# Issuing the k and v loads of two chunk pairs from ScalarE's queue in a gated-recurrence and gated-MLP kernel

## Chip, cores and metric

The kernel runs on one NeuronCore of a Trainium2 chip. The metric is the device time of one execution in microseconds. A "load" below is a transfer from the chip's main memory (HBM) into the core's working memory (SBUF); an engine "issues" a load when its instruction queue hands the transfer over, and the load "lands" when the last part of it has arrived.

## What is computed

The reference is a recurrence over time, for 4 batches and 8 heads of width 48, followed by a gated MLP in which the sequence positions are mixed by a 768 x 768 matrix. Cut to what matters:

```python
def _attn_ref(q, k, v, alpha):              # each (4, 8, 768, 48), float32
    state = np.zeros((B, H, D, D))
    for t in range(S):
        state = alpha[:, :, t, :, None] * state + np.einsum('bhd,bhe->bhde', k[:, :, t], v[:, :, t])
        y[:, :, t] = np.einsum('bhd,bhde->bhe', q[:, :, t], state)
    return y

def _moe_ref(x, w_in, w_spatial, b_spatial, w_out):   # x: (4, 768, 384), w_in: (384, 1024)
    h = np.maximum(x @ w_in, 0.0)
    u, v = h[..., :512], h[..., 512:]
    v_n = (v - mean(v)) / np.sqrt(var(v) + 1e-06)
    v_s = np.einsum('ts,bsd->btd', w_spatial, v_n) + b_spatial[None, :, None]
    return (u * v_s) @ w_out                          # (4, 768, 384)
```

`x` is `y` with the heads side by side.

## The kernel before, in words

The sequence of each batch is cut into six chunks of 128 positions, 24 chunks in all. Within a chunk the recurrence becomes matrix products. With a running sum of log(alpha) (`cum`), k is multiplied by exp(-cum) (`kt`, L449 for pairs and L628 for single chunks) and q by exp(cum) (`qt`, L456 and L638); both are transposed by TensorE and copied to SBUF (`kqT`), multiplied with each other into a 128 x 128 score (`pt`), masked by VectorE (`ptm`, L540 and L696), and multiplied with v (`y`, L556 and L713). A state carried from chunk to chunk (`state`, `sbd`) adds what earlier chunks contribute (L562, L707). `y` is then transposed into `xT`, the input of the MLP. The MLP part (all matmuls on L759) multiplies `xT` by the two halves of `w_in`: half 1 gives v, half 0 gives u; v is normalised, mixed by the transposed `w_spatial`, gated with u and multiplied by `w_out`.

The first six chunks, the whole first batch, are handled in three pairs (`PAIRS`, function `pair(j)` with j = 0, 1, 2): two chunks share each load of alpha, q, k and v. A pair's load is 384 KB, in pieces of 96 floats for 128 partitions and 8 heads (L391). In this text ac0, kc0, qc0 and vc0 are the tiles of alpha, k, q and v for pair 0, and so on to ac2, kc2, qc2, vc2. From chunk 6 on, each chunk has four loads of 192 KB (L585). The loads of `w_in` are two transfers of 768 KB each (L986), half 1 first; they arrive in float32 in `raw_w` and are cast to bf16 by ScalarE, VectorE and GpSimd (L191, L193). All loads, and the stores at the end, are issued by SyncE (SP), except for one tiny bias load by GpSimd.

No scheduler is at work when the kernel is built: every operation is numbered, and the text constant `PLAN` lists the numbers in the order in which they are emitted, each with a letter for its engine (P TensorE, D VectorE, A ScalarE, G GpSimd, S SyncE). `replay` (L111) walks through it and calls each operation's `emit`. Each engine runs what was emitted to it in that order, and every engine waits by semaphores for what it needs. The first part of the plan is:

```python
PLAN = """
G32 Q33 G0 S34 S36 Q35 S38 S96 S40 Q37 S98 D1 S100 S166 A42 Q39 S102 D2 S170
P43:384:384:384:384:384:384:384:384:384:384:384:384 S168 G3 Q97 S4 P54:384 A46 A44 S172 A45 S303 G47 A57 A55 D48 Q41
```

S34, S36, S38 and S40 are ac0, kc0, qc0 and vc0; S96, S98, S100 and S102 are ac1, kc1, qc1 and vc1; S166, S168, S170 and S172 are ac2, kc2, qc2 and vc2. S4 is `w_in` half 1, S303 is the alpha load of chunk 6, and the load of `w_in` half 0 is S9 in the next line. A42 is the logarithm of alpha for pair 0 (`la`, L402); P43 and P54 are the running sums of its even and odd positions (`cum`, L413), and on ScalarE A46, A44 and A45 are the three exponentials that follow the first of them: `bc` (L444), `binvp` (L429, exp(-cum), which `kt` needs) and the one in place (L438, exp(cum), which `qt` needs); A57, A55 and A56 are the same for the odd positions. Numbers after a colon are matmuls on dummy data (`junk`, L183).

Every load counts up one of eight completion semaphores, which are handed out in turn; an issue that reuses one first waits until the load that had it before has landed. Three buffers per tile name (`IO = 3`) let all three pairs' loads be issued without waiting for a pair to be used up.

Of the kernel before, what the change touches and what calls it, by code (L numbers as in the profile page):

```python
# [123 lines left out]
def kernel(  # L124
# [12 lines left out]
    nc = tc.nc  # L137
# [235 lines left out]
    def pair(j):  # L373
# [13 lines left out]
        def load(name, src):  # L387
            def emit(_):
                t = st[name] = io_pool.tile([128, 2, H, D], FP32, name=name).rearrange(
                    "p a h d -> p (a h d)").rearrange("p (h a d) -> p h a d", h=H, a=2)  # L390
                nc.sync.dma_start(  # L391
                    out=t.rearrange("p h a d -> p h (a d)"),
                    in_=src[b, :, t0:t0 + 2 * C, :].rearrange("h (p a) d -> p h (a d)", a=2))
            return emit
# [667 lines left out]
```

## Time and profile before

| what | value |
|---|---|
| median of 3 runs | 150.17 us (150.13 to 150.49) |
| the profiled execution | 149.26 us, of which the span from first to last instruction is 147.5 us |
| TensorE (PE) busy | 140.0 us, 95% of the span |
| VectorE (DVE) busy | 121.9 us, 83% |
| ScalarE (ACT) busy | 105.6 us, 72% |
| GpSimd (POOL) busy | 87.1 us, 59% |
| read from HBM, written to HBM | 23.60 MB, 4.72 MB |
| granted TensorE clock | full speed |

The views of the profile used here are: the page's line of busy tenths, which cuts the span in 40 slices and gives one digit for each (9 is 90% or more), with the DMA engines' share and the GB/s below it; the chain of waits, which goes back from the last instruction and names at each step what released it; the timeline of one engine, with start, length, engine, source line and operation; and the list of who waited for whom. On SP's timeline the length of an issue is the time for which SP was held by it, not the time of the transfer. The trace also records when a load landed on each of the 16 DMA engines; the last of them is the landing time in this text.

### The profile page before, as it was taken

The numbers are of one execution on the slowest core, as the hardware profiler recorded it, in microseconds if no ns is written. First come the engines' busy times: TensorE is split into PE (matmuls) and PEld (weight loads), VectorE is DVE, ScalarE is ACT, GpSimd is POOL, SyncE is SP. The second block draws the span as 40 slices with busy tenths as digits, with TensorE's granted clock in tenths as the row PEclk, the third lists the DMA queues.
The fourth block names the chain that finished last, engine by engine and source line by source line (L and its number), as shares of the span: only waits on it lengthen the run. The fifth ranks groups of instructions, "written<-read, shape, count | busy, mean of one in ns | idle before, by whom it ended". The sixth has DMA issues, their size and how long they took to land.

```text
span 147.5 us, 4398 instructions
## 1 busy us (share of the span) xinstructions
PE 140.0 (95%) x1687; PEld 89.8 (61%) x1687; DVE 121.9 (83%) x266; ACT 105.6 (72%) x264; POOL 87.1 (59%) x149
## 2 busy tenths in 40 slices
PE   6899999989998999999999999999999999999990
PEld 3457766546765766667666757665765766555550
DVE  6688978969999998998996789999898969867611
ACT  3577848788958769899967899899956458950160
POOL 6947468296072978852569877858059897004320
PEclk9999999999999999999999999999999999999999
DMA  4999999989999899899996999997949302250154
GB/s 113 267 261 263 261 287 267 311 213 257 293 203 209 173 209 277 159 207 180 211 225 132 207 224 183 258 231 150 251 138 207 63 4 107 107 213 4 70 198 161
DMA packets 93013, 28.60 MB, mean 194 GB/s; under 512 B 87872, under 2 KB 91456, under 8 KB 92992
## 3 DMA queue, kind: packets, MB, share of 16 engines
q1 hardware_dynamic: 92960, 28.32, 82.9%
q8 instruction: 13, 0.21, 0.7%
q14 instruction: 8, 0.07, 0.2%
q0 software_dynamic: 32, 0.00, 0.0%
HBM read 23.60 MB, written 4.72 MB: 192 GB/s over the span
## 4 chain that ended last, share of the span: by engine, by line
PE 79%; DMA 6%; POOL 4%; ACT 3%; DVE 3%; issue 3%; SPq 0%; POOLq 0%
PE ps L759 51%; DMA raw_w<-in_moe_w_in_dram 6%; PE pt L655 6%; PE pt L685 4%; PE tp L671 2%; PE y L346 2%; PE y L713 2%; PE cum L604 2%; POOL mask L243 2%; PE y L707 2%; PE ps L478 1%; PE ps L769 1%; PE ps L413 1%; PE ps L183 1%; ACT xT L191 1%
## 5 line engine op out<-in xcount | busy, mean ns | idle before, releaser
L759 PE MATMUL ps<-w_spT,vn 128*128 128x384 bf16 x192 | 36.2, 326 | 0.0
L912 POOL TENSOR_TENSOR gT<-vsb,uT 128x384 bf16<-128x384 f32 x28 | 25.6, 925 | 15.7 <-DVE vsb L899 15.1
L628 POOL TENSOR_TENSOR kt<-kc,binv 128x384 bf16<-128x384 f32 x18 | 16.4, 912 | 15.3 <-ACT binv L616 14.6
L696 DVE TENSOR_TENSOR ptm<-pt,mask 128x512 bf16<-128x512 f32 x36 | 23.8, 681 | 0.3 <-PE pt L685 0.2
L759 PEld LDWEIGHTS <-vn 128*128 128x128 bf16 x192 | 17.0, 97 | 9.7 <-issue 0.2
L759 PE MATMUL ps<-xT,w_in 128*128 128x384 bf16 x96 | 19.7, 326 | 0.6 <-ACT xT L191 0.4
L899 DVE TENSOR_TENSOR vsb<-ps,bsp_bc 128x384 f32<-128x384 f32 x31 | 16.5, 550 | 3.6 <-PE ps L759 3.2
L759 PE MATMUL ps<-w_in,xT 128*128 128x512 bf16 x72 | 19.5, 379 | 0.0
L759 PE MATMUL ps<-w_out_sb,gT 128*128 128x384 bf16 x96 | 18.4, 326 | 0.0
L317 POOL TENSOR_TENSOR state<-state,bc 128x192 f32<-128x192 f32 x20 | 10.6, 531 | 10.7 <-DVE state L312 7.2
L191 ACT CAST x_sb<-y 128x384 bf16<-128x384 f32 x24 | 11.5, 481 | 6.3 <-PE y L713 5.0
L821 DVE BATCH_NORM_STATS2 stats<-v_sb 128x6 f32<-128x512 bf16 x20 | 13.7, 683 | 1.4 <-ACT v_sb L197 1.4
L191 ACT COPY xT<-y 128x384 bf16<-128x384 bf16 x24 | 11.5, 481 | 4.1 <-PE y L346 3.4
L197 ACT ACTIVATE v_sb<-ps 128x512 bf16<-128x512 f32 x20 | 11.9, 598 | 2.1 <-PE ps L759 2.1
L193 POOL CAST sbd<-state 64x192 bf16<-64x192 f32 x36 | 12.3, 342 | 1.5
L759 PEld LDWEIGHTS <-w_in 128*128 128x128 bf16 x96 | 8.6, 97 | 6.6 <-issue 1.1
L759 PEld LDWEIGHTS <-gT 128*128 128x128 bf16 x96 | 8.9, 98 | 5.7
L638 DVE TENSOR_TENSOR qt<-qc,cum 128x384 bf16<-128x384 f32 x18 | 9.9, 549 | 2.3 <-ACT cum L633 2.0
L193 DVE COPY kqT<-pt 128x1024 bf16<-128x1024 bf16 x14 | 9.6, 687 | 2.3 <-PE pt L655 2.2
L616 ACT ACTIVATE binv<-cum 128x384 bf16<-128x384 f32 x18 | 8.9, 496 | 3.5 <-PE cum L607 2.9
L191 ACT COPY o_sb<-ps 128x384 f32<-128x384 f32 x9 | 4.3, 483 | 8.8 <-PE ps L759 8.6
L851 DVE TENSOR_SCALAR vn<-v_sb,mvs,rstd 128x512 bf16<-128x512 bf16 x24 | 9.6, 428 | 0.2 <-ACT rstd L844 0.2
(131 smaller groups left out, 298.6 us busy)
## 6 DMA issues: line engine op xcount, KB each, us to landing
ac<-in_alpha_dram SPq DMA_DIRECT2D x18, 192.0 KB, 4.3
kc<-in_k_dram SPq DMA_DIRECT2D x18, 192.0 KB, 3.8
qc<-in_q_dram SPq DMA_DIRECT2D x18, 192.0 KB, 3.8
vc<-in_v_dram SPq DMA_DIRECT2D x18, 192.0 KB, 3.9
raw_w<-in_moe_w_spatial_dram SPq DMA_DIRECT2D x3, 768.0 KB, 5.8
out_dram<-raw_w SPq DMA_DIRECT2D x12, 192.0 KB, 2.3
out_dram<-o_sb SPq DMA_DIRECT2D x9, 192.0 KB, 1.9
raw_w<-in_moe_w_in_dram SPq DMA_DIRECT2D x2, 768.0 KB, 7.9
```

Of the source, the lines that this page charges most:

```text
L191: nc.scalar.copy(out=out, in_=in_)
L193: ENG[eng].tensor_copy(out=out, in_=in_)
L197: nc.scalar.activation(out=out, in_=in_, func=AF.Relu)
L317: ENG[eng].tensor_tensor(out=st["state"], in0=st["state"], in1=st["bc"][:, :, None].to_broadcast([128, HP, D]), op=ALU.mult)
L628: ENG[eng].tensor_mul(out=kt[:, :, :, 0:D], in0=quad(st["kc"]), in1=st["binv"])
L638: nc.vector.tensor_mul(out=qt[:, :, :, 0:D], in0=quad(st["qc"]), in1=st["cv"])
L696: nc.vector.tensor_tensor(out=st["ptm"][:, s], in0=st[f"pt{s}"], in1=mask4, op=ALU.mult)
L759: return lambda ps: nc.tensor.matmul(out=out(ps), lhsT=lhsT(), rhs=rhs(), start=start, stop=stop)
L821: nc.vector.bn_stats(out=stats, in_=d["v_sb"][:, tt, :])
L851: nc.vector.tensor_scalar(out=d["vn"][:, t, :], in0=d["v_sb"][:, t, :], scalar1=d["mvs"][:, t, 0:1], scalar2=d["rstd"][:, t:t + 1], op0=AL ...
L899: nc.vector.tensor_tensor(out=hold["vs"], in0=ps[:, 0:TH], in1=bsp_bc[:, th, :], op=ALU.add)
L912: ENG[eng].tensor_tensor(out=bt[b]["gT"][:, dsl, cols], in0=hold["vs"], in1=bt[b]["uT"][:, dsl, cols], op=ALU.mult)
```

## The change

The loads of k and v for pairs 1 and 2 are issued through `nc.scalar`, so that they stand in ScalarE's instruction queue. Pair 0's four loads, and the alpha and q loads of all pairs, stay with SyncE. `PLAN` is not edited: the four words S98, S102, S168 and S172 keep their places, and so each load stands on ScalarE's queue where its word stands among the A words.

```diff
@@ -388,7 +388,7 @@
             def emit(_):
                 t = st[name] = io_pool.tile([128, 2, H, D], FP32, name=name).rearrange(
                     "p a h d -> p (a h d)").rearrange("p (h a d) -> p h a d", h=H, a=2)
-                nc.sync.dma_start(
+                (nc.scalar if j and name in ("kc", "vc") else nc.sync).dma_start(
                     out=t.rearrange("p h a d -> p h (a d)"),
                     in_=src[b, :, t0:t0 + 2 * C, :].rearrange("h (p a) d -> p h (a d)", a=2))
             return emit
```

In the built program ScalarE's queue now begins: table load, kc1, `la` of pair 0 (L402), vc1, kc2, `bc` (L444), `binvp` (L429), vc2, the exponential in place (L438), and then as before. SP's queue begins: ac0, kc0, qc0, ac1, vc0, qc1, ac2, qc2, `w_in` half 1, the alpha load of chunk 6, `w_in` half 0. No other instruction moves on any engine. Because the semaphores are handed out in the order of building, some waits name other loads than before: ac2's issue waits for the landing of kc0, qc2's for qc0, `w_in` half 1's for ac1 (as before), vc2's for kc1, the alpha load of chunk 6 for vc0 and kc2, and that of `w_in` half 0 for vc1 (before: qc1).

## The prediction

> **What bounds the kernel now.** I read the page first, then the chain of waits, then the timelines of SP and ScalarE for the first 30 us, then the list of waits.
>
> The page's busy lines:
>
> ```profile
> span 147.5 us, 4398 instructions
> ...
> PE   6899999989998999999999999999999999999990
> ...
> DMA  4999999989999899899996999997949302250154
> GB/s 113 267 261 263 261 287 267 311 213 257 293 203 209 173 209 277 159 207 180 211 225 132 207 224 183 258 231 150 251 138 207 63 4 107 107 213 4 70 198 161
> ```
>
> A slice is 3.69 us. TensorE is full from the third slice on, but up to about 29 us that includes dummy matmuls (line 183: 3.59 us of 7 to 20 us, 1.22 us of 20 to 30 us, none later). The DMA engines are full from the second slice, at a flat 261 to 267 GB/s while the pairs' loads run. So the opening is bound by bytes, the rest by TensorE.
>
> The chain of waits says where one becomes the other:
>
> ```profile
> 17.91 0.49 ACT binvp L429
> 18.42 0.47 ACT ps L438
> 18.90 0.41 ACT xT L191
> 19.30 0.17 SPq L585
> 19.52 8.84 DMA raw_w<-in_moe_w_in_dram
> 28.38 1.19 DVE w_in L193 x2
> 29.61 0.68 PE ps L759 x3
> ```
>
> The second half of w_in is issued at 19.52, lands at 28.36, is cast, and the u matmuls begin at 29.61. After that TensorE's own waits sum to 1.2 us, so what is late at 29.61 is late at the end, 118 us later.
>
> SP's timeline shows that its issues queue for bytes:
>
> ```profile
> 0.74 0.43 SPq L391 DMA_DIRECT2D ac<-in_alpha_dram  x1
> 1.23 0.57 SPq L391 DMA_DIRECT2D kc<-in_k_dram  x1
> 1.85 1.09 SPq L391 DMA_DIRECT2D qc<-in_q_dram  x1
> ...
> 5.77 1.44 SPq L391 DMA_DIRECT2D kc<-in_k_dram  x1
> 7.25 1.44 SPq L391 DMA_DIRECT2D qc<-in_q_dram  x1
> ...
> 19.52 3.32 SPq L986 DMA_DIRECT2D raw_w<-in_moe_w_in_dram  x1
> ```
>
> The same 384 KB issue takes 0.43 us with nothing ahead of it and 1.44 us from the fourth on, back to back. The landing events give ac0 4.43, kc0 5.96, qc0 7.46, ac1 8.97, vc0 10.48, kc1 11.98, qc1 13.49, ac2 14.96: one load per 1.50 us (384 KB / 1.50 us = 262 GB/s, the page's rate). Then one DMA engine falls behind by about 1.5 us: vc1 has landed on half of them at 16.19, on the last at 17.82; qc2 follows at 19.24, kc2 20.48, w_in's first half 23.09, vc2 24.40.
>
> ScalarE's timeline, where the moved loads will stand:
>
> ```profile
> 4.52 0.84 ACT L402 ACTIVATE la<-ac 128x768 bf16<-128x768 f32 x1 [2.50 <-DMA ac<-in_alpha_dram]
> 6.21 0.17 ACT L444 ACTIVATE bc<-ps 128x4 f32<-128x4 f32 x1 [0.85 <-PE ps L420]
> 6.29 0.48 ACT L429 ACTIVATE binvp<-ps 128x384 bf16<-128x384 f32 x1
> 6.80 0.47 ACT L438 ACTIVATE ps<-ps 128x384 f32<-128x384 f32 x1
> ```
>
> Between la and bc it is idle for 0.85 us; from bc to 8.24 us it is not. Waits for loads, from the list of waits:
>
> ```profile
> POOL vbp L193 <- DMA vc<-in_v_dram: 3.6, 2, 2.0
> ...
> POOL w_in L193 <- DMA raw_w<-in_moe_w_in_dram: 2.9, 1, 2.9
> ...
> DVE qt L456 <- DMA qc<-in_q_dram: 1.4, 1, 1.4
> ```
>
> (total, times, longest). Pair 0 waits for qc0 and vc0, which stay on SP; pair 1 waits for vc1, which moves; and GpSimd waits 2.9 us for w_in's second half.
>
> [...]
>
> **The change, part by part.**
>
> *Removed from SP:* four issues. kc1, vc1 and kc2 took 1.44, 1.39 and 2.62 us and vc2 0.51, so SP comes to the later ones up to 6.0 us sooner. That is worth nothing by itself: the bytes are unchanged and the rate was already full.
>
> *Bytes reordered.* [...]kc1 (issued near 1 us) goes out beside ac0 and kc0, and vc1 and kc2 follow from about 5 us. Every load left on SP is pushed back by the ScalarE loads that overtake it, at 1.50 us each: qc0 by one (7.46 to 9.0), vc0 by two to three (10.48 to 13.5-15), qc1 by three (kc1 was ahead already: 13.49 to 18.0), ac2 by three (14.96 to 19.5; 20.9 if the lagging engine lags as before), w_in's first half by one (vc2 now ahead: 23.09 to 24.6). w_in's second half has the same bytes ahead as before: 28.36. Slack to set against this: qc0 and vc0 none, ac1 1.0 us (la starts at 9.99), qc1 0.8 (qt at 14.27), ac2 1.05 (la at 16.01).
>
> *Added to ScalarE:* four issues. kc1 stands in idle time, before ac0 has landed: nothing but its bytes, which I take as +0.75 us for ac0 (half a load; bounds 0 and 1.5), so la starts at about 5.2. Behind la stand vc1 and kc2; queued behind them are bc, binvp and everything of pair 0, and waiting for those are GpSimd's kt, VectorE's qt and TensorE's transposes. Behind vc2 stand the in-place exponential (qt waits) and the odd positions. Price of one such issue: 0.43 us at least (SP's[...]), 1.44 + 1.44 = 2.9 us at most[...]. A gain is excluded, since ScalarE issued nothing before. I take 0.45 for itself plus what remains of SP's issue: half of 1.45 the first time, a whole one when the two alternate. vc1 and kc2: 0.7 + 0.45 + 1.45 + 0.45 = 3.0, so bc at 8.2 instead of 6.21; vc2: 1.9, so the in-place exponential at about 10.7 instead of 6.80, and qt at 11.2 instead of 7.59. Pair 0 is then 3.5 us late by either road (exponentials or vc0); the two run side by side and are not summed.
>
> *Waits moved:* w_in's second half now waits for vc1, and chunk 6's alpha for kc2; by the bytes both land before 15 us, and SP is there at 13.5 at the earliest. Nothing[...].
>
> *Given back:* TensorE's upd at 18.43 and the odd scores at 19.38 stood behind vc1 (17.82); now it is early, and pair 1 regains about 1.5 us of its 3.5. Pair 2 begins with ac2: la 19.5-20.9 instead of 16.01. From la to the first kt took 18.39 - 16.01 = 2.4 us by the exponential's end, so kt can start at 21.9-23.3; before, it started at 21.22, held by kc2's landing at 20.48. Pair 2 is late by 0.7 to 2.1 us; I take 1.4. w_in's first half, 1.5 later, delays the v matmuls (24.28) about as much. TensorE works in order, so y at 27.49 and the u matmuls at 29.61 move by 1.4. GpSimd's part is hidden: its 2.92 us of waiting for w_in covers it.
>
> *Sum:* 1.4 us on the chain. The profiled execution of 149.26 us (span 147.5, 1.76 around it) becomes 150.7. It lies 0.91 below the median of the runs; the same 1.4 on the median is 151.6.
>
> **The rivals.**
>
> *ScalarE is held long.* If its issues [...]alternate with SP's, each costs 2.9 us: bc at 5.2 + 5.8 = 11.0, the in-place exponential at 14.4, pair 0's qt late by 6.8. ScalarE then reaches pair 2's la near 22.5, kt starts at 24.9, 3.7 late: 153.9. For it: SP's 1.44 us issues.[...]
>
> *Absorbed.* If the lateness is over by 28.36 (0.7 us or less, inside the gaps of VectorE and ScalarE before it), nothing is left: 150.2. For it: w_in's second half has its place in bytes. Against: TensorE's order.
>
> *Faster: w_in's second half arrives sooner.* SP can issue it up to 6 us sooner. If ScalarE's vc2 goes out behind it instead of ahead, one load less lies before it: 28.36 becomes 26.9, the u matmuls start 1.5 us earlier, 148.7. It decides from the point where vc2's bytes leave after w_in's and pair 2's y is not late. For it: the chain names this landing. Against: la of pair 2 hangs on ac2, which gets later in every order.
>
> That the change doesn't do what it says can be left aside: the built order shows the four loads on ScalarE.
>
> **How the numbers follow.** Forecast (0.9 to 2.2 us later) 0.46; ScalarE held long 0.24; absorbed 0.10; faster 0.20. A measurement can tell about 0.3%, 0.45 us, from no change: faster 0.20, same 0.10, slower 0.70. The range runs from inside the faster case (149.2, leaving out some 0.12) to beyond the held case (154.6, leaving out some 0.06).
>
> **What would show it.** Right: ac0 near 5.2, qc0 near 9, vc0 at 13 to 15, ac2 at 19 or later, la of pair 2 as late; ScalarE's vc1, kc2 and vc2 issues over 0.45 us; qt of pair 0 near 11; w_in's second half still near 28.4; u matmuls near 31. Wrong: SP's loads landing as before[...], a rate well over 262 GB/s before 16 us (two issuers move more), or w_in's second half before 27.5.

## The result, and the profile after

| | before | after |
|---|---|---|
| median | 150.15 us (149.41 to 150.49, 4 runs) | 160.13 us (158.63 to 160.25, 4 runs) |
| ratio, 95% interval | | 1.0649 (1.0574 to 1.0724) |
| profiled execution / its span | 149.26 / 147.5 us | 158.63 / 156.9 us |
| granted TensorE clock, mean | 1.000 | 0.935 |
| first `y` matmul of pair 0, 1, 2 starts | 14.35, 21.30, 27.49 us | 18.72, 28.70, 37.18 us |
| u matmuls start | 29.61 us | 38.98 us |

The change costs 10 us: the time lies far above the 151.6 us forecast, and outside its range. The u matmuls start 9.37 us later, and the profiled execution is longer by the same 9.37 us: as the prediction said of this place, what is late there is late at the end. So everything is lost in the first 39 us. Here and below, a ratio leaves out executions that took over 1.5% more than the fastest of the same program; the medians and ranges hold them all.

The page's busy lines of the kernel after. PEclk is the TensorE clock that was granted, in tenths of full speed (9 is full, 5 is half); a slice is 3.92 us:

```profile
span 156.9 us, 4387 instructions
...
PE   6597899999899899999999999999999999999990
...
PEclk9969755559999999999999999999999999999999
DMA  4999994055899979999989999899699700450054
GB/s 116 270 261 261 265 323 168 2 181 128 231 261 216 198 151 189 187 276 205 198 166 194 197 195 199 178 249 221 129 231 270 161 6 0 170 214 22 22 213 168
```

In the kernel before, the PEclk row is nines from end to end. Here it falls. The trace's own events give the times: full from 4.01 us, half from 7.42, full from 10.83, half from 17.66, full from 34.73 to the end. The row and the mean count the time ahead of the first event as full, which it is not: in the kernel before, a dummy matmul of 384 columns takes 527 ns up to the first event, at 4.27 us, and 326 ns after it. So "full speed" in the table of before holds from 4.27 us on. Meanwhile the DMA row drops to 0 in the eighth slice (27.5 to 31.4 us): the loads are all there, and TensorE is behind them.

The chain of waits of the kernel after, up to the u matmuls:

```profile
8.75 6.49 issue
...
15.26 0.96 POOL vbp L193 x2
...
16.27 0.37 PE tp L509 x12
...
18.79 0.75 PE y L556 x16
...
28.77 0.75 PE y L556 x16
...
37.25 0.50 PE y L556 x16
...
38.27 0.67 PE ps L759 x3
```

`w_in`'s second half, on the chain before, is no longer on it. The longest piece up to there is now the 6.49 us in which GpSimd stood still for vc0 (the list of waits names it below); from there it goes through the cast of v and then stays on TensorE, but for a copy of `xT` of 0.5 us. And the same 16 `y` matmuls take 0.75 us at half clock and 0.50 us at full.

SyncE's and then ScalarE's timelines, to set against those of before:

```profile
3.12 2.69 SPq L391 DMA_DIRECT2D ac<-in_alpha_dram  x1
...
8.83 3.26 SPq L391 DMA_DIRECT2D ac<-in_alpha_dram  x1
...
19.77 1.44 SPq L986 DMA_DIRECT2D raw_w<-in_moe_w_in_dram  x1
```

```profile
5.51 0.84 ACT L402 ACTIVATE la<-ac 128x768 bf16<-128x768 f32 x1 [3.49 <-DMA ac<-in_alpha_dram]
5.53 0.37 ACTq L391 DMA_DIRECT2D vc<-in_v_dram  x1
5.93 0.63 ACTq L391 DMA_DIRECT2D kc<-in_k_dram  x1
...
7.21 2.46 ACTq L391 DMA_DIRECT2D vc<-in_v_dram  x1
7.28 0.49 ACT L429 ACTIVATE binvp<-ps 128x384 bf16<-128x384 f32 x1
9.72 0.47 ACT L438 ACTIVATE ps<-ps 128x384 f32<-128x384 f32 x1 [1.96 <-issue]
```

On SP, ac1's issue took 2.69 us (1.25 before) and ac2's 3.26 (1.44 before). On ScalarE, vc1 and kc2 were handed over in 1.0 us and were done at 6.56, while ScalarE waited for TensorE up to 7.21 in any case: they held nothing. vc2 took 2.46 us, and the in-place exponential behind it stood for 1.96 us.

From the list of waits (total, times, longest):

```profile
POOL vbp L193 <- DMA vc<-in_v_dram: 6.5, 1, 6.5
...
DVE qt L456 <- ACT ps L438: 4.6, 2, 4.1
```

Landing times, from the trace of each, in us:

| load | ac0 | kc0 | qc0 | ac1 | vc0 | kc1 | qc1 | ac2 | vc1 | qc2 | kc2 | w_in half 1 | vc2 | w_in half 0 |
|---|---|---|---|---|---|---|---|---|---|---|---|---|---|---|
| before | 4.43 | 5.96 | 7.46 | 8.97 | 10.48 | 11.98 | 13.49 | 14.96 | 17.82 | 19.24 | 20.48 | 23.09 | 24.40 | 28.36 |
| after | 5.42 | 7.63 | 9.14 | 11.50 | 15.21 | 6.28 | 18.16 | 20.89 | 12.15 | 22.33 | 15.45 | 24.45 | 18.44 | 27.21 |

The clock events of one trace lie 3.41 us or a multiple of it apart; 3.41 us is called a step here. What TensorE did in some of these steps (columns: stretch; length; busy time and count of PE, PEld, DVE, ACT, POOL; clock; DMA share; GB/s), first after:

```profile
10.83:14.24 3.41, 3.39 (x48) 1.77 (x46) 3.08 (x7) 2.49 (x5) 0.00 (x0) 1.00 1.28 261
14.24:17.66 3.42, 1.94 (x47) 1.50 (x47) 1.28 (x4) 1.90 (x6) 2.31 (x5) 1.00 1.30 265
17.66:21.07 3.41, 3.41 (x53) 3.01 (x50) 2.53 (x7) 1.67 (x5) 2.66 (x7) 0.50 1.19 286
...
27.89:31.31 3.42, 3.42 (x48) 2.62 (x47) 2.04 (x6) 1.01 (x3) 3.30 (x8) 0.50 0.01 2
31.31:34.73 3.42, 3.42 (x40) 2.22 (x37) 1.58 (x3) 1.85 (x4) 0.77 (x1) 0.50 0.52 149
```

and before:

```profile
14.50:17.91 3.41, 3.41 (x81) 2.63 (x78) 3.07 (x9) 2.92 (x9) 1.26 (x5) 1.00 1.18 258
17.91:21.32 3.41, 2.91 (x65) 1.98 (x63) 2.48 (x5) 2.31 (x6) 2.20 (x6) 1.00 0.98 276
```

In the step before the fall TensorE was busy for 1.94 of 3.42 us, since it waited for the cast of vc0. In the next it is busy all the time but gets 53 matmuls done where before it did 65 to 81; and h2_fill_trim below, with the same loads and the clock kept up, did 89 in the same stretch:

```profile
17.66:21.07 3.41, 3.39 (x89) 2.86 (x87) 3.37 (x9) 2.33 (x5) 2.86 (x7) 1.00 1.19 289
```

"Busy" is no measure of work when the clock is halved.

In all 15 traces the clock is either half or full, and its events lie 3.41 us or a multiple of it apart. What the profile calls busy does not bring it back by itself: here five steps passed, each busy from end to end (3.41 of 3.41 us), before the clock came back. And what it calls busy did not hold it: the clock fell although the 3.42 us before the fall held 1.94 us of matmuls.

### The profile page after: what moved, and what is told of

Its sections match the earlier page's. It is cut to its first block, busy times and chain, and to the rows that moved or that the text cites. A ratio compares the mean times of both kernels' runs of the same rounds, so it can differ in the third digit from the quotient of the medians.

```text
span 156.9 us, 4387 instructions
## 1 busy us (share of the span) xinstructions
PE 146.8 (94%) x1674; PEld 94.6 (60%) x1687; DVE 121.8 (78%) x266; ACT 105.8 (67%) x264; POOL 86.8 (55%) x149
## 4 chain that ended last, share of the span: by engine, by line
PE 79%; DVE 7%; issue 7%; POOL 4%; ACT 1%; ACTq 0%; POOLq 0%
PE ps L759 47%; PE pt L655 5%; PE pt L685 4%; PE y L346 3%; PE y L556 3%; PE ps L478 2%; PE tp L671 2%; PE y L713 2%; PE cum L604 2%; POOL mask L243 2%; PE y L707 2%; PE tp L509 2%; DVE vn L851 1%; PE pt L529 1%; PE ps L413 1%
## 5 line engine op out<-in xcount | busy, mean ns | idle before, releaser
L759 PE MATMUL ps<-w_spT,vn 128*128 128x384 bf16 x192 | 36.2, 326 | 0.0
L696 DVE TENSOR_TENSOR ptm<-pt,mask 128x512 bf16<-128x512 f32 x36 | 23.9, 681 | 0.3 <-PE pt L685 0.2
L759 PEld LDWEIGHTS <-vn 128*128 128x128 bf16 x192 | 17.0, 97 | 9.7 <-issue 0.2
L759 PE MATMUL ps<-xT,w_in 128*128 128x384 bf16 x96 | 19.7, 326 | 0.5 <-ACT xT L191 0.4
L759 PE MATMUL ps<-w_in,xT 128*128 128x512 bf16 x59 | 18.0, 392 | 0.8 <-ACT xT L191 0.2
L759 PE MATMUL ps<-w_out_sb,gT 128*128 128x384 bf16 x96 | 18.4, 326 | 0.1
L759 PEld LDWEIGHTS <-w_in 128*128 128x128 bf16 x96 | 8.6, 97 | 6.3 <-issue 1.1
L759 PEld LDWEIGHTS <-gT 128*128 128x128 bf16 x96 | 8.9, 97 | 5.7
L540 DVE TENSOR_TENSOR ptm<-pt,mask 128x512 bf16<-128x512 f32 x12 | 7.7, 686 | 3.7 <-PE pt L529 3.7
```

The lines of the kernel that those rows point to most:

```text
L696: nc.vector.tensor_tensor(out=st["ptm"][:, s], in0=st[f"pt{s}"], in1=mask4, op=ALU.mult)
L759: return lambda ps: nc.tensor.matmul(out=out(ps), lhsT=lhsT(), rhs=rhs(), start=start, stop=stop)
```

## The experiments

The theory that this trace suggests: the loads that overtake vc0, qc1 and ac2 make pair 0 and pair 2 late; TensorE runs dry, loses its clock, and most of the 10 us is the half clock. Rivals: ScalarE's hold (its compute stands behind its issues) is what costs; two issuing engines are slower than one; the clock is a mere witness, and the lateness of the loads is worth 10 us by itself.

Two measures tell them apart in each run: the start of the u matmuls and the mean granted clock, both of the profiled execution unless a range is given. The mean counts the time ahead of the first event as full. Each ratio is against runs of the kernel before on the same chip (medians of 149.37 to 150.15 us).

| run | what differs | median, us | ratio (95%) | clock | u starts, us |
|---|---|---|---|---|---|
| after | | 160.13 | 1.0649 (1.0574 to 1.0724) | 0.935 | 38.98 |
| e2_sp_order | SyncE issues all, in the order of after | 159.7 | 1.066 (1.0588 to 1.0731) | 0.935 | 40.00 |
| f2_vc0_late | before, vc0 moved back | 160.34 | 1.0734 (1.0685 to 1.0783) | 0.925 | 40.66 |
| f3_q_alpha_late | before, qc1, ac2, qc2 moved back | 159.66 | 1.0684 (1.0644 to 1.0723) | 0.930 | 40.17 |
| f4_no_dummy | before without dummy matmuls | 154.87 | 1.037 (1.0326 to 1.0414) | half up to 31.0 us | 35.02 |
| e1_fill | after, 49 dummy matmuls more | 156.0 | 1.044 (1.0393 to 1.0487) | 0.996 | 36.20 |
| f1_fill_before | before, the same 49 | 154.35 | 1.0337 (1.029 to 1.0384) | 0.998 | 34.63 |
| g2_fill_light | after, 39 more | 155.5 | 1.0394 (1.0332 to 1.0456) | 0.999 | 35.28 |
| g1_fill_one_wait | after, 25 more at the first three waits | 153.91 | 1.0298 (1.0232 to 1.0363) | 0.988 | 34.20 |
| h2_fill_trim | after, 17 more at these waits | 152.52, 153.01, 157.86, 161.21 | none | 1.000, 0.999, 0.962, 0.920 | 32.88 (first) |
| h1_hold_alone | before, ScalarE held for 2.1 us | 150.19 | 1.0045 (1.0021 to 1.0068) | 1.000 | 30.40 |
| e3_kc1_only | only kc1 on ScalarE | 150.39 | 1.007 (1.0043 to 1.0098) | 0.995 | 30.73 |
| e4_act_late | the four on ScalarE, later | 153.61 | 1.0252 (1.0173 to 1.0331) | 0.941 to 0.989 | 37.00 (at 0.941) |
| g3_act_late2 | three on ScalarE, later | 156.25 | 1.0455 (1.0406 to 1.0504) | 0.956 | 36.95 |

The dummy matmuls and copies change no result. The table counts matmuls by the record. The expectations count otherwise: e1_fill's 98 takes in 49 weight loads, the others count entries in the plan, of which each "384" at P65 becomes two matmuls of 192 columns, and where they say two more ahead of the transposes, the edit has three.

### Is it the engine or the order?

e2_sp_order leaves ScalarE out of it: all twelve loads of the pairs stand on SyncE, in about the order in which they landed after the change.

```diff
-G32 Q33 G0 S34 S36 Q35 S38 S96 S40 Q37 S98 D1 S100 S166 A42 Q39 S102 D2 S170
-P43:... S168 G3 Q97 S4 P54:384 A46 A44 S172 A45 S303 ...
+G32 Q33 G0 S34 S36 Q35 S98 S38 S96 Q37 S102 D1 S168 S40 A42 Q39 S172 D2 S100
+P43:... S166 S170 G3 Q97 S4 P54:384 A46 A44 A45 S303 ...
```

> The kernel before, all loads on SyncE, in about the order in which they landed in the changed kernel: ac0 kc0 kc1 qc0 ac1 vc1 kc2 vc0 vc2 qc1 ac2 qc2, then w_in. ScalarE issues nothing. If the order of the loads is the cause (starving TensorE and dropping its clock): vc0 lands near 15 us, the clock falls as in the changed kernel, 157 to 161 us. If ScalarE's being held by its issues is the cause: 150 to 153 us.

Measured: 159.7 us, clock 0.935, v of pair 0 cast from 15.04 us. The page's clock row, and the in-place exponential from ScalarE's timeline, at 6.78 us, as early as before:

```profile
PEclk9999555559999999999999999999999999999999
```

```profile
6.78 0.47 ACT L438 ACTIVATE ps<-ps 128x384 f32<-128x384 f32 x1
```

The order alone gives the whole loss; neither ScalarE's hold nor a second issuing engine is needed for it.

h1_hold_alone is the other half: the loads of before, and copies of 2.13 us that no one needs in front of the in-place exponential.

```diff
+                if j == 0 and par == 0:
+                    for n in (768, 768, 256):
+                        nc.scalar.copy(out=w_spT[:, 0, 0:n], in_=st["ac"].rearrange("p h a d -> p (h a d)")[:, 0:n])
                 nc.scalar.activation(
```

> The kernel before, its loads untouched, with three dummy copies on ScalarE (some 2 us, into a buffer that is overwritten later) ahead of the in-place exponential of pair 0: ScalarE's hold alone. Theory (the lateness of the loads lets TensorE run dry and its clock falls; the hold is no cause): the in-place exponential and qt of pair 0 come about 2 us later, pair 0's waits take up most of it, the clock stays full, 149.5 to 151.5 us. Rival (the hold by itself lets TensorE run dry between 8 and 18 us): the clock falls to half before 20 us and the time is 154 to 160 us.

Its ScalarE timeline:

```profile
6.69 0.48 ACT L429 ACTIVATE binvp<-ps 128x384 bf16<-128x384 f32 x1
7.06 2.13 ACT L440 CAST w_spT<-ac 128x768 bf16<-128x768 f32 x3
9.10 0.47 ACT L441 ACTIVATE ps<-ps 128x384 f32<-128x384 f32 x1
```

The exponential came 2.3 us later (9.10 against 6.80), the u matmuls 0.79 us later, and the median rose by 0.82 us (150.19 against 149.37): the hold alone costs 0.8 of its 2.1 us. In 16 of 17 executions the time was 149.77 to 150.81 us; one had a clock of 0.919 and took 158.80. So the rival is not dead as a risk, but it isn't the cause: after is at 0.925 to 0.935 in all four of its executions.

e3_kc1_only moves the first of the four only:

```diff
-                nc.sync.dma_start(
+                (nc.scalar if j == 1 and name == "kc" else nc.sync).dma_start(
```

> Only kc1 is issued by ScalarE, before la of pair 0, where ScalarE is idle; vc1, kc2 and vc2 stay on SyncE. No hold of ScalarE on the way of pair 0. By the order of bytes ac0, qc0, ac1 and vc0 land 1 to 1.5 us later than before. Theory of order: 1 to 2 us slower, 151 to 152.5, if the clock stays full; up to 157 if the lateness of 1.5 us is enough for the clock to fall. Theory of ScalarE's hold: 150.2, no change.

Measured 150.39 us; u matmuls 1.12 us later, clock 0.995. One load overtakes, the others come up to 1.5 us later (v of pair 0 is cast from 12.04 instead of 10.53), and from its first event, at 10.51 us, the clock stays full. Ahead of that it was at half, longer than before: the dummy matmuls there take 527 ns. One of the six executions took 748.12 us at a clock of 1.000; the record doesn't say why, and nothing here rests on it.

### Which late load?

Two runs on SyncE alone. f2_vc0_late takes only vc0 back, to the eighth place; f3_q_alpha_late keeps it and puts qc1, ac2 and qc2 last.

```diff
 f2_vc0_late
-G32 Q33 G0 S34 S36 Q35 S38 S96 S40 Q37 S98 D1 S100 S166 A42 Q39 S102 D2 S170
-P43:... S168 G3 ...
+G32 Q33 G0 S34 S36 Q35 S38 S96 Q37 S98 D1 S100 S166 A42 Q39 S40 D2 S102
+P43:... S170 S168 G3 ...
 f3_q_alpha_late
-G32 Q33 G0 S34 S36 Q35 S38 S96 S40 Q37 S98 D1 S100 S166 A42 Q39 S102 D2 S170
-P43:... S168 G3 Q97 S4 P54:384 A46 A44 S172 A45 ...
+G32 Q33 G0 S34 S36 Q35 S38 S96 S40 Q37 S98 D1 S102 S168 A42 Q39 S172 D2 S100
+P43:... S166 S170 G3 Q97 S4 P54:384 A46 A44 A45 ...
```

> The kernel before, all loads on SyncE, vc0 moved from fifth to eighth place, behind ac2 (landing near 15 us as in the changed kernel); kc1, qc1 and ac2 land 1.5 us earlier than before. If vc0 is the load whose lateness counts (GpSimd's first kt of pair 1 and TensorE's upd stand behind its cast): GpSimd waits to 15 us, the clock falls near 17 us, 155 to 160 us. If it is the lateness of qc1, ac2 and qc2: 150 to 152 us.

> The kernel before, all loads on SyncE; vc0 keeps its place and lands at 10.5 us, then come kc1 vc1 kc2 vc2 and only then qc1 (near 18 us) and ac2 (19.5 to 21 us), qc2. If vc0 is what counts: 150 to 152 us. If the lateness of qc1 and ac2 is enough by itself (VectorE's qt of pair 1 at 18 instead of 14.3 us): 154 to 159 us, with or without a fall of the clock.

The clock rows of their pages, f2_vc0_late first:

```profile
PEclk9996555557999999999999999999999999999999
```

```profile
PEclk9999555558999999999999999999999999999998
```

Each costs the full 10 us by itself (160.34 and 159.66), and the clock is half for 24 us (13.45 to 37.34) and 20 us (16.52 to 36.99). In the second, pair 0's `y` starts at 14.37, as before, and pair 1's wait for q is enough; VectorE's timeline shows it, and TensorE stood behind it for 4.89 us:

```profile
19.22 1.02 DVE L456 TENSOR_TENSOR qt<-qc,ps 128x384 bf16<-128x384 f32 x2 [4.86 <-DMA qc<-in_q_dram]
```

The two latenesses don't add up: e2_sp_order has both and costs no more (159.7). Whichever comes first drops the clock, and then the price is paid. I had looked for one load as the cause; either of two is enough by itself.

### What is half the clock worth?

f4_no_dummy turns the question round: the loads of before, but every dummy matmul taken out of the plan, so that nothing fills TensorE's waits.

```diff
-P43:384:384:384:384:384:384:384:384:384:384:384:384 S168 ...
+P43 S168 ...
```

> The kernel before without any dummy matmul of the plan; loads as before. It shows what the clock is worth with the loads in good order. If half clock in the opening costs about half of its length: clock at half for much of 4 to 25 us, 153 to 157 us. If the opening is bound by the loads and TensorE has room: 150 to 151 us whatever the clock does.

Measured 154.87 us, 5.1 over its 149.77. The page's clock row is all nines, since the first event, of a full clock, comes at 31.02 us only; but the running sums of 384 columns took 510 ns between 11 and 31 us (331 ns before), so the clock was half up to then:

```profile
L413 PE MATMUL ps<-la,le_pair 128*128 128x384 bf16 x6 | 2.6, 510 | 0.0
```

Half a clock up to 31 us instead of 4.3, with all loads in time and less to do for TensorE, costs 5.1 us.

The page's groups of matmuls by shape let the loss be added up. In after, over the 17.07 us from 17.66 to 34.73, and before, at full clock over 11 to 29 us:

```profile
L556 PE MATMUL y<-vbp,ptm 64*128 64x48 bf16 x64 | 3.3, 213 | 0.0
L478 PE MATMUL ps<-ident,qt 128*128 128x128 bf16 x16 | 2.5, 311 | 0.0
...
L413 PE MATMUL ps<-la,le_pair 128*128 128x384 bf16 x3 | 1.3, 511 | 0.0
```

```profile
L556 PE MATMUL y<-vbp,ptm 64*128 64x48 bf16 x80 | 2.9, 181 | 0.0
...
L413 PE MATMUL ps<-la,le_pair 128*128 128x384 bf16 x6 | 1.7, 331 | 0.0
L478 PE MATMUL ps<-ident,qt 128*128 128x128 bf16 x16 | 1.6, 221 | 0.0
```

A group's busy time (the first number behind the bar) divided by its count, and times the count after, is what it would have taken at full clock: 2.9 x 64/80 = 2.3 for L556 against 3.3, 1.6 against 2.5 for this half of L478. In the same way for all forms in both lists, dummies apart (L478 1.8, L556 1.0, L346 0.7, L759 0.7, L413 0.65, L529 0.6, L509 0.5, L562 0.45), half clock cost TensorE 6.4 us in that stretch.

### Is the clock a cause or a witness?

If the clock is kept up while the loads stay late, a cause must give the time back. e1_fill adds 49 dummy matmuls all over the first 30 us of after, and f1_fill_before adds the same to before.

```diff
-D244 G49 Q101 P105 D74 G60 P116 A106 D75 P65 A117 ...
+D244 G49 Q101 P105 D74 G60 P116 A106 D75 P65:384:384:384:384:384:384:384 A117 ...
-D126 P83 A174 D72 P135 A84 G111 P175 ...
+D126 P83:384:384 A174 D72 P135:384:384 A84 G111 P175:384:384 ...
```

> The changed kernel with 98 more dummy matmuls and their weight loads on TensorE, put where it waits between 4.7 and 35 us; loads and all else as in the changed kernel. Theory A (the late loads starve TensorE, the granted clock falls to half from 17.66 to 34.73 us, and most of the 9.4 us of loss is work done at half clock): clock 1.0 through this stretch, 152 to 155 us. Theory B (the order of the loads alone costs the 9 us, the clock is only a sign of it): clock 1.0 or not, 158 us or more. If the clock stays at half in spite of the filling, the run tells nothing of B.

> The kernel before with the same extra dummy matmuls as in e1_fill. If the filling is itself a good part of e1_fill's 6.4 us over the kernel before: 151 to 153 us. If it lies in TensorE's waits here too: 149.5 to 150.5 us, and e1_fill's 6.4 us is then the order of the loads at full clock.

The clock stayed full and after fell to 156.0 us, a little above the 152 to 155 expected. But in before the filling itself cost 4.6 us (154.35 against 149.77), more than expected of it, so that the first of these runs could not say what the order costs alone. The two together say 1.8 us (6.4 over its before against 4.6), but with filling on both sides that may hide part of it. A lighter filling and one around the single wait were next:

```diff
 g1_fill_one_wait (g2_fill_light has these and more, from P112 to P200)
-P43:(12 x 384)   P50:(7 x 384):96   P65
+P43:(16 x 384)   P50:(10 x 384):96   P65:(9 x 384)
```

> The changed kernel with 28 extra dummy matmuls, those of g1 and one at each of the later waits up to 33 us (e1_fill has 45; the 98 rows said of it counted the weight loads too). It bounds the price of the order of the loads at full clock. If order and clock add up (clock 5 us as in the kernel without dummy matmuls): clock full, 154 to 155.5 us. If the order costs what was forecast, 1.4 us, and the clock the rest: 151 to 153 us. If the clock falls in spite of the lighter filling: 157 us or more, and the question stays open.

> The changed kernel with 15 extra dummy matmuls: 4 ahead of pair 0's running sums, 2 ahead of its transposes, 9 ahead of the upd matmuls that wait for vc0 (idle from 14.6 to 15.8 us in the changed kernel). If this one wait is what drops the clock for the whole of 17.66 to 34.73 us: clock full from about 11 us, 152 to 156 us. If the clock falls at the next wait (for qc1, near 19 us) all the same: 157 to 160 us.

With 25 dummies where TensorE waits, the changed kernel is 4.5 us over its before (153.91 against 149.43) instead of 10.0; 14 more of them, further on, cost 1.6 us again. g1 still fell to half for one step, and one of its four executions took 156.36 us at a clock of 0.974. In its trace those at the wait for v ran from 14.81 to 17.45, 1 us past the cast of v. h2_fill_trim ends them in time:

```diff
-P43:(16 x 384)   P50:(10 x 384):96   P65:(9 x 384)
+P43:(16 x 384)   P50:(10 x 384):96   P65:(5 x 384)
```

> The changed kernel with its dummy matmuls sized to the waits: 4 more ahead of pair 0, 2 more behind its first scores, and 5 of 384 columns at the wait for v of pair 0 where an earlier run had 9, so that they end near 16.3 us, when v is cast. Theory (at a full clock the order of the loads costs 3 to 3.5 us): 152.5 to 153.5 us, clock 0.98 or more, u matmuls near 33. If the forecast's 1.4 us is the order's own price at full clock: 151 to 152. If the shorter fill doesn't hold the clock: it falls at about 18 us for five steps or more, 156 to 160 us.

This one program tells most by being uneven: four executions, 152.52 and 153.01 us at a clock of 1.000 and 0.999, 157.86 at 0.962 and 161.21 at 0.920. Same instructions in the same order, and the time follows the clock: 5 us and more between having it and not. (Only the first has a trace, so that the loads landed alike in the other three is not shown.) The filling holds the clock by so little that some executions lose it, so no median stands for this run. Its profiled execution kept it (152.52 us), and shows what the order costs at a full clock. Part of its chain:

```profile
20.46 0.85 ACT la L402
...
24.95 0.61 PE y L556 x16
...
31.15 0.50 PE y L556 x16
...
32.17 0.67 PE ps L759 x3
```

The u matmuls start at 32.88, 3.27 us later than before, and the execution is 152.52 - 149.26 = 3.26 us longer. The three pairs' first `y` start at 18.44, 24.88 and 31.08 us: 4.1, 3.6 and 3.6 us late. The dummies added at the wait for v end at 15.45 us, before the cast of v lets TensorE go on at 15.94, so they are not part of this; those further ahead left the in-place exponential at 9.63 us (9.72 in after). So the 9.37 us of the change are 3.3 us of late loads (with whatever ScalarE's hold adds, which this run has too) and 6.1 us of half clock; the 6.4 us added up from the shapes and the 5.1 us of f4_no_dummy are of the same size.

These runs also narrow down what work holds the clock. The busy time doesn't tell it: g2_fill_light kept the full clock after a step with 2.19 us of matmuls, g1_fill_one_wait lost it after one with 2.37, and got it back after a single step at half, as busy as the five of after:

```profile
12.78:16.19 3.41, 2.19 (x30) 1.52 (x30) 1.32 (x3) 1.95 (x4) 0.08 (x1) 1.00 1.29 262
```

```profile
11.88:15.29 3.41, 2.37 (x43) 1.57 (x43) 1.75 (x3) 1.65 (x3) 0.00 (x0) 1.00 1.29 261
15.29:18.71 3.42, 3.42 (x49) 2.69 (x47) 0.53 (x2) 1.41 (x5) 2.05 (x4) 0.50 1.27 263
```

What differs is the tile of a matmul, the first two numbers behind the names in the lists of shapes: 128*128 for a dummy, 64*128 for `y` (L556), 48*64 for the scores (L529). An estimate from the traces: back-to-back dummies of 384 columns start 0.163 us apart at full clock and 0.320 us at half, so these times, scaled by a matmul's columns and by its tile's share of 128 x 128, give its work, and a step can be compared with one full of such dummies. In the first 42 us of the 15 traces, the eight steps after which the clock fell held 0.19, 0.24, 0.24, 0.26, 0.26, 0.31, 0.33 and 0.38 of that, and the 116 steps after which it stayed full 0.40 or more. At half, it came back after steps with 0.75 or more and stayed at half after steps with up to 0.84. In after, the step before the long fall held 0.31, the first four at half 0.61 to 0.70, and the fifth, with the 512-column matmuls of `w_in`, 0.88; in g1_fill_one_wait the one step at half, with its dummies, held 0.89. This was found by sorting what the traces hold; no run was made to test it.

### Can the move be saved by issuing later?

e4_act_late and g3_act_late2 put the same loads on ScalarE's queue where they overtake less, by moving the words in the plan; g3 leaves kc1 on SyncE.

```diff
 g3_act_late2
-P43:... S168 G3 Q97 S4 P54:384 A46 A44 S172 A45 S303 G47 A57 A55 D48 Q41
-S9 A56 D58 P50:... P52 A51 D59 P61:128 Q99 D53 A62 P63:256 ...
-D244 ... A118 D78
+P43:... G3 Q97 S4 P54:384 A46 A44 A45 S303 G47 A57 A55 D48 Q41
+S9 A56 S102 D58 P50:... P52 A51 D59 P61:128 Q99 D53 A62 S168 P63:256 ...
+D244 ... A118 S172 D78
```

> The same four loads on ScalarE, but each behind pair 0's exponentials: kc1 behind the last of them (8.2 us), vc1 before la of pair 1 (10 us), kc2 behind the exponentials of pair 1 (14 us), vc2 before la of pair 2 (16 us). Pair 0's loads are overtaken by nothing. If issuing from ScalarE is harmful in itself: over 152 us. If only what it overtakes and holds counts: clock full, vc1 and kc2 land before 17.82 and 20.48 us, 149 to 150.5 us; slower by up to 2 us if kc1 lands after 12.3 us.

> vc1, kc2 and vc2 from ScalarE, each behind the exponentials of pair 0 or 1 (8.2, 9.7 and 13.5 us); kc1 stays on SyncE in its place. Nothing that pair 0 or pair 1's scores need is overtaken. If only the order of landing counts: ac2 and qc2 within 1 us of before, clock full, 149 to 150.5 us, the same as before within 0.5%. If issues from ScalarE cost by themselves: 151 us or more.

In e4, whose four executions leave it unclear whether it is over 2% slower, kc1 was issued at 8.22 and landed 6.2 us later, behind what SyncE had queued; GpSimd's `kt` waited 3.02 us for it, and the clock was 0.941 to 0.989 by execution (156.66 to 152.68 us). g3's ScalarE timeline:

```profile
8.17 0.43 ACTq L391 DMA_DIRECT2D vc<-in_v_dram  x1
9.53 0.37 ACTq L391 DMA_DIRECT2D kc<-in_k_dram  x1
...
13.33 0.37 ACTq L391 DMA_DIRECT2D vc<-in_v_dram  x1
19.43 0.84 ACT L402 ACTIVATE la<-ac 128x768 bf16<-128x768 f32 x1 [2.18 <-DMA ac<-in_alpha_dram]
```

The three issues cost ScalarE 1.2 us together, and still `la` of pair 2 came at 19.43 instead of 16.01, because vc1 and kc2 went past ac2, which landed at 19.40 instead of 14.96. Both runs missed what I expected of them, and both times lie where issues that cost by themselves would put them. They don't show such a cost, though: in neither did the loads land in time, which was the condition, and in both the clock fell (at 17.12 and 19.89 us). A version in which ScalarE issues and nothing comes late was not found. No version here beats the kernel before.

## Why the prediction was wrong, step by step

*SP relieved: nothing.* Right as to the worth. The relief itself did not come either: SP reached `w_in`'s second half at 19.77 us, no sooner than before (19.52).

*Bytes reordered.* That kc1 goes out beside ac0 and kc0 was my estimate, which no trace of before shows; it landed at 6.28 us, between ac0 (5.42) and kc0 (7.63). The landings were right, within 0.4 us: qc0 9.14 (forecast 9.0), vc0 15.21 (13.5 to 15), qc1 18.16 (18.0), ac2 20.89 (19.5, or 20.9 with the lagging engine), `w_in`'s first half 24.45 (24.6). Only the second half landed at 27.21 instead of 28.36, which was one of the named signs of being wrong. That is the arrival on which the rival "faster" was built, and it was worth nothing, since pair 2 was late.

*Added to ScalarE.* About right, for another reason than given: `la` at 5.51 (5.2), `bc` at 7.21 (8.2), the in-place exponential at 9.72 (10.7), `qt` at 10.23 (11.2). vc1 and kc2, priced at 3.0 us behind `la`, cost nothing, since ScalarE waits there anyway; vc2 cost 2.46 us instead of 1.9. That an issue of ScalarE waits for what remains of SP's was my estimate, and it was not shown: kc2 was done at 6.56 while SP's issue of vc0 ran from 5.85 to 7.30. ScalarE held long, as a rival, is refuted. Pair 0's `y` is 4.4 us late after and 4.1 in h2_fill_trim, forecast 3.5: by vc0, as e2_sp_order shows, not "by either road".

*Waits moved: nothing.* Right: on SP's timeline no gap over 0.13 us stands before either of the two issues (17.85 and 19.77).

*Given back.* This step failed, in two ways. The smaller: pair 1 was to regain 1.5 of 3.5 us and pair 2 to be 1.4 late. At full clock (h2_fill_trim) pair 1 regained 0.5 us (3.6 late), and pair 2 nothing more. I priced pair 2 from its own loads, `la` and 2.4 us to the first `kt`. `la` came as forecast, at 20.46; but in GpSimd's queue that `kt` stands behind pair 1's state, as the GpSimd timeline of h2_fill_trim shows:

```profile
23.44 0.51 POOL L317 TENSOR_TENSOR state<-state,bc 128x192 f32<-128x192 f32 x1 [2.15 <-DVE state L312]
24.01 0.73 POOL L193 CAST sbd<-state 64x192 bf16<-64x192 f32 x2
24.82 1.78 POOL L449 TENSOR_TENSOR kt<-kc,binvp 128x384 bf16<-128x384 f32 x2
```

It began at 24.82, not at 21.9 to 23.3. Pair 1's lateness is handed on by the order of the queues, and the term of 1.4 us is 3.3.

The larger: the step let lateness pass through TensorE at its full speed. I had counted the dummy matmuls in the busy row and read them as filler; I took no step to ask what they were for, and what TensorE does when GpSimd's wait for v, behind which it stands, grows from 2.0 to 6.5 us. With the clock at half, pair 1 did not regain but lost another 3.0 us (4.4 late to 7.4), and pair 2 another 2.3 (9.7). That is the 6.1 us which no case of the prediction held.

*Sum.* 1.4 us became 3.3 us of late loads and 6.1 us of half clock. That the u matmuls' start carries over to the end one for one was right: in each of the 14 traces beside that of before, the two differ by 0.03 us at most.

Not settled: what exactly the clock follows. The estimate above, by columns and tile, sorts all falls and most returns, but no run was made with only that changed. And two executions of h2_fill_trim lost the clock without a trace to say after which step.

## What to carry to other kernels

Moving a load to another engine's queue is a change of order among transfers: price it by what it overtakes, then follow the late tile through each engine's order, not through its own inputs alone. Where a plan holds dummy matmuls or a clock row is full all along, treat the clock as a resource: here loads whose lateness was worth 3.3 us cost 6.1 us more by the half clock that followed. Read the granted clock before the chain, check it on the duration of one shape of matmul, and never read a busy TensorE as a working one while it is half.

## What the runs showed of the hardware

- In the 15 traces the clock moved only between full and half, at times 3.41 us or a multiple of it apart, and one wait was enough: in after, 1.94 us of matmuls in a step of 3.42 us didn't hold it. By the estimate above, steps with 0.38 or less of the work of back-to-back 128 x 128 dummies lost it, steps with 0.40 or more kept it.
- The duration on record of a matmul doesn't double at half clock (384 columns 331 to 511 ns, 128 columns 221 to 311, 48 columns 181 to 213), but the distance between starts does: back-to-back dummies of 384 columns start 0.163 us apart at full clock and 0.320 at half.
- The mean granted clock can hide a half: f4_no_dummy reads 1.000 with 31 us at half, as the time ahead of the first clock event counts as full.
- Two issuing engines left the rate at 261 to 270 GB/s (slices two to five of the page, up to 19.6 us), where one had 261 to 267 (slices two to five, up to 18.4 us). The two shared about equally: ac1 and vc1 landed at 11.50 and 12.15 us, vc0 and kc2 at 15.21 and 15.45, qc1 and vc2 at 18.16 and 18.44. qc0, which kc1 overtook, came 1.68 us later.
- An issue on ScalarE took 0.37 to 0.63 us, but 2.46 us when SP had two long ones running beside it (ac2's issue went from 1.44 to 3.26 us on SP as well); ScalarE's compute behind it in the queue stood still, what had been handed over ahead of it (`binvp`, at 7.28) did not.
- In h2_fill_trim, the same program took 152.52 us at a clock of 1.000 and 161.21 at 0.920. The kernel before stands near that edge too: one of its runs beside g3_act_late2 had a clock of 0.966 and took 152.93 us.
